# An FFT convolution beside a gated feed-forward net: new buffer homes, a spectrum copied out before it is multiplied, and an order planned with a price on TensorE tile-mode changes

## The chip, the cores and the metric

The kernel runs on one core of a Trainium2 chip. The metric is device time in microseconds (us), the median of several executions; lower is better. The profile shows one execution, engine by engine: PE is TensorE (matmul; PEld its weight loads), DVE is VectorE, ACT is ScalarE, POOL is GpSimd, and SP only issues DMAs here.

## What is computed

S = 2048 rows, D = 640 channels, F = 1728; inputs and outputs are bf16.

```python
xn = layernorm(A_q)                                   # over D
g  = silu(gelu(xn @ B_w1 + B_b1) @ B_w2 + B_b2)       # feed-forward net
k_shift[s] = sum_t A_k[s + t - 3] * A_shift_k[:, 3 - t]   # 4 taps, zero padded in front
kv = k_shift * A_v
y  = irfft(rfft(kv, 2S) * rfft(A_ssm_k, 2S))[:S]      # long convolution over s, per channel
out = A_q + (xn * (y + kv * A_ssm_D)) * g
```

## The kernel before

**Layout.** Row s = 16p + j lies in partition p. The channels are cut into two halves h of 320. Work on rows goes by four chunks c (4 of the 16 j each); the net runs chunk by chunk, the convolution half by half.

**The convolution** is a Fourier transform in two steps, each a matmul against a table of sines.
- `kt` transposes the filter `A_ssm_k` (in `kf_sb`) into `kT` (L580): 16 transposes for each of 5 blocks of 128 channels.
- `f1_pair` (L622) is the first step: two matmuls of 128x320 for each j, against tables WA and WB. It is done for the filter (kinds f1k0, f1k1, from `kT`) and for the product kv (f1u0, f1u1). Each result is evicted to a staging buffer `io` and stored to DRAM (scrK, scrU), from where it comes back regrouped.
- `kv_unit` (L642, L649, L652) makes the product on DVE: for 4 of the 16 j of one half, four multiplies by a tap, three adds, one multiply by V, each 128x1280 in bf16. Its scratch is the tile `GAB`, where the tables of the last step are put later by a DMA transpose (L732). So the tables come after all eight units.
- `middle` (L773, L803, L816) works on 8 groups for each half. `f2k`: the filter's second step, 4 matmuls on 64x64 quarters of the array, twice a group; the result is evicted to `kk`, and a DMA puts a copy with the partitions exchanged beside it (swap, L790). `f2u`: the same for the product, read from `uin`. `prod` (L803): DVE multiplies this spectrum by both versions in `kk`. `i1` (L816): 8 quarter matmuls turn the product back; its result `cs` is evicted and stored to scrC by POOL (L822).
- `last` (L834, L835, L842) loads `cab` from scrC (it waits for all 8 groups of the half), does 4 matmuls of 128x320 and multiplies by xn. `finish` (L539, L541) adds A_q and stores.

**The net.** `layer_norm` (statistics L483, 1/sqrt on POOL L490, normalizing L493), `x_transpose` (DMA transposes, L510), `ffn1` (L522: 5 matmuls of 128x512, gelu on ACT L527; 14 for each chunk), `ffn2` (L557: 14 matmuls of 128x320, silu on ACT L561, multiply into xn on DVE L565; 8 for each chunk).

**Buffers that matter here.** PSUM has two banks `psf` for the net and three double banks `psa` for all else. `w2_sb` shares its memory with `kf_sb`, so w2 is loaded only when all 5 blocks of the filter are transposed:

```python
w2_sb = kf_sb[:].rearrange("p t s -> p (t s)")[:, 0:FT * D]...      # L289
load(ld, F * D * 2, writes=[w2_b], extra=list(kf_b.users), n=3)     # L606
```

`kT` lies over the memory of rows chunks 2 and 3 (`xreg`, L292), so these chunks are loaded when the last filter pair is done. The K and V rows of both halves have homes of their own (`k_all`, `v_all`), which after use serve as `uin`, `cs` and `cab`. The tables' integer scratch lies in `hx[1]`, later the net's second hidden buffer.

**The order.** Every step is recorded as an `op` with its engine, a cost and a kind. `schedule` is a list planner: of the steps that are ready it takes the one that can start first, ties broken by a number for its kind from the table DUE (two numbers a kind, first and last step of it). An eviction may go to ACT or DVE (`"ACT|DVE"`). The steps are then issued in that order, and each engine runs its own in order: a step that waits holds back all behind it on its engine. DMAs are issued by SP in order, too.

Of the kernel before, what the change touches and what calls it, by code (L numbers as in the profile page):

```python
# [9 lines left out]
F32 = mybir.dt.float32  # L10
# [5 lines left out]
P = 128  # L16
# [50 lines left out]
TABLE_LOAD = 1.28  # L67

class Plan:
# [4 lines left out]
    def op(self, eng, cost, fn, reads=(), writes=(), mods=(), hold=(), kind="", table=None, dma=0, rate=360e3, extra=()):  # L74
# [3 lines left out]
        o.fn, o.kind, o.table, o.dma, o.rate = fn, kind, table, dma, rate  # L78
# [33 lines left out]
    def schedule(self):  # L112
# [21 lines left out]
        dma_free, table = 0.0, None  # L134
# [4 lines left out]
        while ready:  # L139
            best = None  # L140
            for o in ready:
# [19 lines left out]
                for e in o.engs:  # L161
# [23 lines left out]
            if e == "ACT" and o.table is not None:  # L185
                table = o.table
            if o.dma:
# [44 lines left out]
def kernel(  # L232
# [119 lines left out]
    def load(fn, nbytes, reads=(), writes=(), extra=(), n=1):  # L352
        nload[0] += 1
        if len(loads) >= 3:
            extra = list(extra) + [loads[-3]]
# [526 lines left out]
```

## Time and profile before

| | |
|---|---|
| median of 3 executions | 227.08 us (226.32 to 228.15) |
| the profiled execution | 226.49 us, span in its profile 224.3 us |
| busy PE / DVE / ACT / POOL | 194.7 / 173.4 / 147.2 / 25.2 us |
| mean granted PE clock | 0.96 |
| moved by DMA | 58.67 MB, 262 GB/s |

The span goes from the first to the last instruction; 2.2 us of the device time lie around it. The text takes a row apart at its first use.

### The profile page before, as it was taken

Reading aid. Unit: us, or ns where it says so; the run is one execution under the profiler, and the core shown is the slowest. Engines: PE = TensorE matmul, PEld = TensorE weight load, DVE = VectorE, ACT = ScalarE, POOL = GpSimd, SP = SyncE. Lnnn points to the kernel's source line nnn. Section 1 sums busy time; section 2 is a strip of 40 time slices with the busy share of each in tenths; the row PEclk is TensorE's granted clock in tenths of the full one; section 3 lists DMA queues with packets and bytes.
Section 4 is the critical chain, followed back from the end, with each engine's and each line's share of the span. In section 5 each row is a group of like instructions: output and inputs, shape, how many; then the busy total and the mean of one; then the engine's idle time right before and its main releaser. Section 6 shows DMA issues by size and latency. Waiting matters only on the chain.

```text
span 224.3 us, 4150 instructions
## 1 busy us (share of the span) xinstructions
PE 194.7 (87%) x1521; PEld 105.5 (47%) x1521; DVE 173.4 (77%) x297; ACT 147.2 (66%) x225; POOL 25.2 (11%) x36
## 2 busy tenths in 40 slices
PE   4523996992899989999999899999899999999992
PEld 1521253541567633446665443343334555657771
DVE  6999989979999978653989666557387697882594
ACT  6397778687278886887766797777646758742110
POOL 8060000002000000110111301110111100220000
PEclk9985599999699999999999999999999999999999
DMA  6999999999995799999959999897999852535953
GB/s 172 358 304 198 303 353 317 377 346 354 225 329 178 250 288 270 267 337 311 346 171 176 262 256 340 245 314 219 294 382 330 248 164 91 177 91 187 358 163 113
DMA packets 63614, 58.67 MB, mean 262 GB/s; under 512 B 17453, under 2 KB 55145, under 8 KB 63594
## 3 DMA queue, kind: packets, MB, share of 16 engines
q1 hardware_dynamic: 62026, 53.16, 81.1%
q0 software_dynamic: 1536, 5.24, 7.3%
q8 instruction: 12, 0.20, 0.4%
q14 instruction: 8, 0.07, 0.1%
q10 hardware_dynamic: 32, 0.01, 0.0%
HBM read 31.14 MB, written 18.35 MB: 221 GB/s over the span
## 4 chain that ended last, share of the span: by engine, by line
PE 67%; DMA 20%; DVE 6%; SPq 2%; ACT 2%; issue 1%; POOL 1%; DVEq 0%; ACTq 0%; POOLq 0%
PE psf_106 L557 14%; PE psf_105 L557 13%; PE psf_105 L522 11%; PE psf_106 L522 10%; DMA w_sb<-in_B_w_dram 5%; DMA kf_sb<-in_B_w_dram 4%; DMA k_all<-scrC_67 3%; DMA kf_sb<-in_A_ssm_k_dram 3%; PE psa_107 L816 2%; PE psa_107 L622 2%; DMA hx_93<-xreg 2%; PE psa_109 L773 2%; PE psa_108 L622 2%; PE psa_108 L773 2%; DMA xreg<-in_A_q_dram 2%; PE psa_109 L622 2%
## 5 line engine op out<-in xcount | busy, mean ns | idle before, releaser
L522 PEld LDWEIGHTS <-w_sb 128*128 128x128 bf16 x280 | 25.3, 99 | 36.2 <-issue 13.1
L557 PEld LDWEIGHTS <-hx_93 128*128 128x128 bf16 x224 | 21.9, 100 | 15.1 <-issue 6.2
L642 DVE TENSOR_TENSOR GAB<-k_all,w_exp 128x1280 bf16<-128x1280 bf16 x32 | 26.0, 820 | 0.5
L557 PEld LDWEIGHTS <-hx_94 128*128 128x128 bf16 x224 | 21.3, 98 | 9.5 <-issue 1.0
L557 PE MATMUL psf_106<-kf_sb,hx_93 128*128 128x320 bf16 x112 | 17.8, 315 | 4.5 <-DMA kf_sb<-in_B_w_dram 4.5
L522 PE MATMUL psf_105<-hx_93,w_sb 128*128 128x512 bf16 x70 | 18.5, 398 | 1.8 <-DMA w_sb<-in_B_w_dram 1.8
L649 DVE TENSOR_TENSOR GAB<-GAB 128x1280 bf16<-128x1280 bf16 x24 | 19.6, 817 | 0.2
L522 PE MATMUL psf_106<-hx_93,w_sb 128*128 128x512 bf16 x70 | 18.5, 397 | 0.9 <-DMA hx_93<-xreg 0.9
L522 PE MATMUL psf_105<-hx_94,w_sb 128*128 128x512 bf16 x70 | 17.5, 380 | 0.5 <-ACT hx_94 L527 0.5
L522 PE MATMUL psf_106<-hx_94,w_sb 128*128 128x512 bf16 x70 | 17.5, 380 | 0.5 <-ACT hx_94 L527 0.5
L557 PE MATMUL psf_105<-kf_sb,hx_93 128*128 128x320 bf16 x112 | 16.6, 300 | 0.0
L557 PE MATMUL psf_106<-kf_sb,hx_94 128*128 128x320 bf16 x112 | 16.6, 299 | 0.0
L557 PE MATMUL psf_105<-kf_sb,hx_94 128*128 128x320 bf16 x112 | 16.6, 299 | 0.0
L483 DVE BATCH_NORM_STATS2 stats<-xreg 128x6 f32<-128x320 bf16 x32 | 13.7, 471 | 2.0 <-DMA xreg<-in_A_q_dram 2.0
L822 POOL DMA_DIRECT2D scrC_67<-v_all x8 | 6.4, 797 | 76.7 <-ACT v_all L313 73.9
L527 ACT ACTIVATE hx_93<-psf_105,b_f 128x512 bf16<-128x512 f32 (+1 forms) x14 | 9.7, 690 | 7.5 <-PE psf_105 L522 7.5
L527 ACT ACTIVATE hx_94<-psf_105,b_f 128x512 bf16<-128x512 f32 (+1 forms) x14 | 9.6, 686 | 7.4 <-PE psf_105 L522 7.3
L622 PEld LDWEIGHTS <-WA 128*128 128x128 bf16 x64 | 6.4, 100 | 13.0 <-ACT WA L452 7.8
L527 ACT ACTIVATE hx_94<-psf_106,b_f 128x512 bf16<-128x512 f32 (+1 forms) x14 | 9.6, 687 | 4.1 <-PE psf_106 L522 3.8
L773 PEld LDWEIGHTS <-F2m 64*64 64x64 bf16 x256 | 6.0, 104 | 13.4 <-issue 12.6
L561 ACT ACTIVATE sl_102<-psf_106 128x320 bf16<-128x320 f32 x6 | 2.6, 437 | 13.7 <-PE psf_106 L557 13.7
L490 POOL TENSOR_TENSOR rstd<-veps,mhalf 128x4 f32<-128x4 f32 x4 | 5.5, 1366 | 51.0 <-DVE veps L487 51.0
(188 smaller groups left out, 405.7 us busy)
## 6 DMA issues: line engine op xcount, KB each, us to landing
kf_sb<-in_A_ssm_k_dram SPq DMA_DIRECT2D x5, 512.0 KB, 6.3
k_all<-in_A_k_dram SPq DMA_DIRECT2D x4, 640.0 KB, 7.9
v_all<-in_A_v_dram SPq DMA_DIRECT2D x4, 640.0 KB, 8.6
kk_95<-kk_95 SPq DMA_DIRECT2D x16, 160.0 KB, 4.4
kk_96<-kk_96 SPq DMA_DIRECT2D x16, 160.0 KB, 3.8
k_all<-scrU_65 SPq DMA_DIRECT2D x8, 320.0 KB, 4.1
scrC_67<-v_all POOLq DMA_DIRECT2D x8, 320.0 KB, 4.6
k_all<-scrU_66 SPq DMA_DIRECT2D x8, 320.0 KB, 5.4
```

Of the source, the lines that this page charges most:

```text
L483: nc.vector.bn_stats(out=stats[:, c, j, h, :], in_=x_b[c].v[:, j, h * H:(h + 1) * H])
L490: op("POOL", 0.96, lambda e: nc.gpsimd.tensor_tensor(out=rstd[:, c, :], in0=veps[:, c, :], in1=mhalf[:], op=ALU.pow), reads=[ve_b[c], mh_b ...
L522: nc.tensor.matmul(out=o, lhsT=w1_sb[:, t, ft * P:(ft + 1) * P], rhs=xnT_b[c].v[:, :, t, :], start=(t == 0), stop=(t == DT - 1))
L527: op("ACT", 0.575, lambda e: nc.scalar.activation(out=hT_b[c].v[0:M, ft, :], in_=ps.v[0:M, :], func=ACT.Gelu_apprx_tanh, bias=b1_f[0:M, ft ...
L557: nc.tensor.matmul(out=ps.v[:, 0:H], lhsT=hT_b[c].v[0:M, ft, q * P:(q + 1) * P], rhs=w2_sb[0:M, ft, hs], start=(ft == 0), stop=(ft == FT - 1))
L561: op("ACT", 0.32, lambda e: nc.scalar.activation(out=sl.v[:], in_=ps.v[:, 0:H], func=ACT.Silu), reads=[ps], writes=[sl], kind="f2_%d" % c, ...
L622: nc.tensor.matmul(out=ps.v[:, c, 0:H], lhsT=W[:, 2 * i + j, :], rhs=src(2 * i + j), start=True, stop=True)
L642: nc.vector.tensor_tensor(out=out_, in0=k_all[:, h, r + 3 - j:r + 3 - j + KR, :], in1=w_exp[:, j, None, hs].to_broadcast([P, KR, H]), op=A ...
L649: op("DVE", 0.735, lambda e, t=t: nc.vector.tensor_tensor(out=a.v, in0=a.v, in1=t.v, op=ALU.add), reads=[t], writes=[a], kind="kv%d" % h)
L773: nc.tensor.matmul(out=ps.v[t * Q:t * Q + Q, u, 0:H], lhsT=W[u * Q:u * Q + Q, :], rhs=src[u * Q:u * Q + Q, 2 * i + t, :], start=True, stop ...
L816: nc.tensor.matmul(out=psc.v[u * Q:u * Q + Q, t, 0:H], lhsT=W[t * Q:t * Q + Q, :], rhs=p12.v[t * Q:t * Q + Q, 2 * a + u, :], start=(a == 0 ...
L822: op("POOL", 1.04, lambda e: nc.gpsimd.dma_start(out=by_group(scrC[h], g), in_=cs.v), reads=[cs], writes=[scrC_b[h][g]], kind="cst%d" % h, ...
```

## The change

1. **Homes.** w2 gets its own memory; the filter `kf_sb` now lies in `hx[1]`, and the tables' integer scratch in w2's. w2's load waits for the tables only. `kT` moves from the rows chunks 2 and 3 to the memory of the second half's K and V (`kv_t[1]`): chunks 2 and 3 may load at any time, and K and V of the second half load only after the last filter pair.
2. **The product's spectrum.** `f2u`'s result is evicted in place into `uin` (ACT or DVE), and `prod` reads it from there in bf16. Before, `prod` read PSUM in f32. `f2u` no longer waits for the swapped filter spectrum, nor for a free staging buffer.
3. **Staging** buffers `io`: 4 for 3.
4. **Normalizing** is x * rstd + (-mean * rstd), with one small DVE step more for each chunk, so that ACT can do it as well as DVE.
5. **The planner** knows PE's tile mode: a change between full-array steps and quarter steps (f2k, f2u, i1) costs 0.095 us and a number of its own in DUE. The costs of some steps, DMA issues above all, are set anew, loads hold one of 3 tokens where they followed the load three before, and all of DUE is new. So the order is new everywhere.

```diff
+MODE_SWITCH = 0.095
...
+                    if e == "PE" and o.mode != mode:
+                        c += MODE_SWITCH
+                        p -= self.due["mode"][0]
...
-    kf_sb = sb.tile([P, DT, S], BF16, name="kf_sb")
-    w2_sb = kf_sb[:].rearrange("p t s -> p (t s)")[:, 0:FT * D].rearrange("p (t d) -> p t d", t=FT)
+    nmr = sb.tile([P, NCH, CH], F32, name="nmr")
+    w2_sb = sb.tile([P, FT, D], BF16, name="w2_sb")
...
-    kT = xreg[:, NCH:].rearrange("p a b d -> p (a b) d")
-    k_all = sb.tile([P, 2, NJ + 3, H], BF16, name="k_all")
-    v_all = sb.tile([P, 2, NJ, H], BF16, name="v_all")
+    kv_t = [sb.tile([P, NK + NJ * H], BF16, name="kv%d" % h) for h in range(2)]
+    kT = kv_t[1][:, 0:NJ * D].rearrange("p (n d) -> p n d", d=D)
...
+    kf_sb = hx[1][:].rearrange("p (t s) -> p t s", t=DT)
...
-    io_t = [sb.tile([P, 4, H], BF16, name="io%d" % i) for i in range(3)]
+    io_t = [sb.tile([P, 4, H], BF16, name="io%d" % i) for i in range(4)]
...
-             writes=[x_b[c]], extra=list(kT_b.users) if c >= 2 else [])
+             writes=[x_b[c]])
...
-             writes=v_b[h].parts[8 * i:8 * i + 8])
+             writes=v_b[h].parts[8 * i:8 * i + 8], extra=list(kT_b.users) if h else [])
...
-        load(ld, F * D * 2, writes=[w2_b], extra=list(kf_b.users), n=3)
+        load(ld, F * D * 2, writes=[w2_b], extra=tab_users, n=3)
...
-            def prod(e, i=i, ps=ps, p12=p12):
-                nc.vector.tensor_tensor(out=p12.v[:].rearrange("p (a u) c -> p a u c", a=2),
-                                        in0=ps.v[:, None, :, 0:H].to_broadcast([P, 2, 2, H]),
-                                        in1=kk.v[:, i], op=ALU.mult)
-
-            op("PE", T2, lambda e, i=i, ps=ps: quads(ps, F2m, uin.v, i), reads=[uin, F2_b, kk], writes=[ps],
-               hold=[p12], kind="f2u%d" % h)
-            op("DVE", 1.4, prod, reads=[ps, kk], writes=[p12], kind="prod%d" % h)
+            op("PE", T2, lambda e, i=i, ps=ps: quads(ps, F2m, uin.v, i), reads=[uin[2], F2_b], writes=[ps],
+               kind="f2u%d" % h, mode=1)
+            op("ACT|DVE", EV, lambda e, i=i, ps=ps: evict(e, uin.v[:, 2 * i:2 * i + 2, :], ps.v[:, :, 0:H]), reads=[ps], writes=[uin[i]],
+               kind="f2u%d" % h)
+
+            def prod(e, i=i, p12=p12):
+                us = uin.v[:, 2 * i:2 * i + 2, :]
+                nc.vector.tensor_tensor(out=p12.v[:].rearrange("p (a u) c -> p a (u c)", a=2),
+                                        in0=us.rearrange("p u c -> p (u c)")[:, None, :].to_broadcast([P, 2, 2 * H]),
+                                        in1=kk.v[:, i].rearrange("p a u c -> p a (u c)"), op=ALU.mult)
+
+            op("DVE", 0.735, prod, reads=[uin[i], kk], writes=[p12], hold=[cs], kind="prod%d" % h)
```

**What moves on the engines.** PE's 274 steps (a step is one recorded group of matmuls) are the same ones. Along its order the tile mode changes 112 times before and 76 times now: quarter steps stand in longer runs between the net's. DVE has 53 casts for 19 (the 34 more are evictions), ACT 111 for 113, and ACT loads its function table 10 times for 12. Three places follow.

SP, the DMA queue, near the start, before: the rows from the last filter block (L372) to the load of the second half's last V piece. `k_all` rows L392 to L394 and `v_all` rows L400 here are the second half's K and V; L384 loads rows chunk 1, L627 stores filter pairs.

```order
17 L372 DMA kf_sb<-in_A_ssm_k_dram 128x2048
18 L392 DMA k_all<-in_A_k_dram 112x3x320
19 L393 DMA k_all<-in_A_k_dram 15x3x320
20 L394 DMA k_all<-in_A_k_dram 128x8x320
21 L380 DMA w_sb<-in_B_w_dram 128x5x576
22 L400 DMA v_all<-in_A_v_dram 128x8x320
23 L627 DMA scrK_63<-io_99 128x1280
24 L627 DMA scrK_63<-io_101 128x1280
25 L394 DMA k_all<-in_A_k_dram 128x8x320
26 L384 DMA xreg<-in_A_q_dram 128x2560
27 L400 DMA v_all<-in_A_v_dram 128x8x320
```

SP in the change: first the same stretch, from the first transposes of xn (L528) to w2 (L623; `kv_91` is the first half's K and V, L394 loads rows chunks 2 and 3).

```order
13 L528 DMA_TRANSPOSE hx_94<-xreg 128x10x128 x2
14 L382 DMA hx_95<-in_A_ssm_k_dram 128x2048
15 L410 DMA kv_91<-in_A_v_dram 128x8x320
16 L394 DMA xreg<-in_A_q_dram 128x2560
...
20 L394 DMA xreg<-in_A_q_dram 128x2560
21 L404 DMA kv_91<-in_A_k_dram 128x8x320
22 L382 DMA hx_95<-in_A_ssm_k_dram 128x2048
23 L646 DMA scrK_63<-io_100 128x1280
24 L646 DMA scrK_63<-io_102 128x1280
25 L623 DMA w_sb<-in_B_w_dram 128x13x640
```

All three pieces of w1 (L390) now stand ahead of this, and w2 stands behind two filter stores whose data are evicted by DVE and ACT. Farther on in SP's order of the change stand the second half's K and V (`kv_92`), around the last store of a filter pair (L646, `scrK_64`):

```order
58 L410 DMA kv_92<-in_A_v_dram 128x8x320
59 L646 DMA scrK_64<-io_101 128x1280
60 L402 DMA kv_92<-in_A_k_dram 112x3x320
61 L403 DMA kv_92<-in_A_k_dram 15x3x320
62 L404 DMA kv_92<-in_A_k_dram 128x8x320
63 L410 DMA kv_92<-in_A_v_dram 128x8x320
```

They have moved from the first fifth of the queue to its middle. On DVE, before, the same multiplies and adds of the second half's first unit stood right behind the first half's, with no work of `middle` between. In the change they stand among products (L830) and evictions (L324) of the first half's `middle`:

```order
157 L324 CAST kv_91<-psa_110 128x640 x2
158 L661 TENSOR_TENSOR GAB<-kv_92,w_exp 128x1280 x3
159 L668 TENSOR_TENSOR GAB<-GAB 128x1280
...
162 L830 TENSOR_TENSOR io_100<-kv_91,kk_96 128x1280
163 L830 TENSOR_TENSOR io_101<-kv_91,kk_96 128x1280
164 L661 TENSOR_TENSOR GAB<-kv_92,w_exp 128x1280
165 L324 CAST kk_96<-psa_108 128x640
...
168 L671 TENSOR_TENSOR kv_92<-GAB,kv_92 128x1280
169 L324 CAST kv_91<-psa_110 128x640
```

From row 158 to the last such multiply, row 211, DVE has 32 instructions of the second half's units, 10 products, 9 evictions and 5 short multiplies of the net (L583).

DVE near the start, in the change: rows chunk 1 is normalized (L508, its statistics some rows ahead) before the second unit of the first half (`kv_91`) begins, and behind it stand the two evictions for the filter stores that w2 follows.

```order
62 L661 TENSOR_TENSOR GAB<-kv_91,w_exp 128x1280
63 L501 SCALAR_TENSOR_TENSOR nmr<-mv,rstd 128x4
64 L671 TENSOR_TENSOR kv_91<-GAB,kv_91 128x1280
65 L508 TENSOR_SCALAR xreg<-xreg,rstd,nmr 128x640 x4
66 L661 TENSOR_TENSOR GAB<-kv_91,w_exp 128x1280
67 L324 CAST io_100<-psa_108 128x640
68 L668 TENSOR_TENSOR GAB<-GAB 128x1280
69 L324 CAST io_102<-psa_110 128x640
```

Before, neither chunk 1's statistics nor an eviction of a pair stood among the first two units:

```order
62 L642 TENSOR_TENSOR GAB<-k_all,w_exp 128x1280
63 L652 TENSOR_TENSOR v_all<-GAB,v_all 128x1280
64 L642 TENSOR_TENSOR GAB<-k_all,w_exp 128x1280
65 L649 TENSOR_TENSOR GAB<-GAB 128x1280
66 L313 COPY xreg<-psa_108 128x8x128
67 L642 TENSOR_TENSOR GAB<-k_all,w_exp 128x1280
68 L649 TENSOR_TENSOR GAB<-GAB 128x1280
```

More of the change, by code (lines that the diff above doesn't have):

```diff
@@ L72, in __init__, with op @@
         self.due = due
-    def op(self, eng, cost, fn, reads=(), writes=(), mods=(), hold=(), kind="", table=None, dma=0, rate=360e3, extra=()):
+    def op(self, eng, cost, fn, reads=(), writes=(), mods=(), hold=(), kind="", table=None, dma=0, rate=360e3, mode=0, extra=()):
         o = Op()
@@ L133, in schedule @@
         free = {"PE": 1.0, "ACT": 1.0, "DVE": 1.0, "POOL": 1.0, "SP": 1.0}
-        dma_free, table = 0.0, None
+        dma_free, table, mode = 0.0, None, 0
         for p in {b.pool for o in ops for b in o.allocs}:
@@ L186, in schedule @@
                 table = o.table
+            if e == "PE":
+                mode = o.mode
             if o.dma:
@@ L594 @@
                reads=[dD_b], writes=[kT_b[2 * u] for u in range(d0 // P, d1 // P)], kind="kt")
-    load_k(1, 0)
-    load_v(1, 0)
+    op("POOL", 0.5, lambda e: nc.gpsimd.memset(hT_t[1][FLAST:FLAST + 1, FT - 1, :], 1.0), writes=[], kind="ones1",
+       extra=list(kf_b.users))
     load_x(1)
+    load_x(2)
+    load_x(3)
     def load_w2():
@@ L666 @@
             f1_pair(i, h, k_src(h), k_dep(h), scrK, scrK_b, "f1k%d" % h)
-    load_x(2)
-    load_x(3)
+    op("POOL", 1.0, lambda e: nc.gpsimd.memset(k_all[1][0:1, 0:3, :], 0.0), writes=[halo_b[1]], kind="halo1",
+       extra=list(kT_b.users))
+    for i in range(2):
+        load_k(1, i)
+        load_v(1, i)
     for h in range(2):
```

96 lines of the change are left out of this document (51 added, 45 removed), and 42 rows, old and new, of the table DUE.

## The prediction

> **What bounds the kernel now.** I read the page first (span, busy times, granted clock), then a table of stages, then PE's waits, then the chain.
>
> ```profile
> span 224.3 us, 4150 instructions
> PE 194.7 (87%) x1521; PEld 105.5 (47%) x1521; DVE 173.4 (77%) x297; ACT 147.2 (66%) x225; POOL 25.2 (11%) x36
> PEclk9985599999699999999999999999999999999999
> ```
>
> ```profile
> 0.00:57.00 57.00, 35.22 (x200) 19.29 (x201) 51.95 (x120) 40.97 (x54) 10.74 (x18) 0.87 1.05 310
> 57.00:224.30 167.30, 159.44 (x1322) 86.25 (x1320) 121.46 (x178) 106.24 (x171) 14.45 (x18) 0.99 0.83 245
> 80.00:140.00 60.00, 58.20 (x480) 28.90 (x479) 42.79 (x69) 45.43 (x74) 6.93 (x8) 1.00 1.00 275
> 57.00:80.00 23.00, 23.00 (x164) 15.05 (x163) 22.24 (x35) 16.29 (x28) 0.00 (x0) 0.95 0.88 240
> 200.00:220.00 20.00, 19.81 (x148) 13.99 (x144) 12.30 (x26) 3.90 (x9) 0.75 (x1) 1.00 0.65 216
> ```
>
> The columns are the stretch, its length, busy PE, PEld, DVE, ACT and POOL with counts, PE clock, DMA share, GB/s. The kernel has two parts. Up to 57 us PE is busy 35 of 57 while DVE (52) and the DMA (share 1.05) are full. After 57 us PE has 159.4 of the 163 us to its last matmul (219.85, below), so it lacks 3.4 us there: what counts is its work and when it starts. PE's waits (who waited <- for whom: us in all, times, longest) and the chain that ended last (start, us, what):
>
> ```profile
> PE psa_108 L622 <- ACT WA L452: 7.7, 1, 7.7
> PE psf_106 L557 <- DMA kf_sb<-in_B_w_dram: 4.5, 1, 4.5
> PE psf_105 L522 <- DMA w_sb<-in_B_w_dram: 1.8, 1, 1.8
> PE psa_108 L834 <- DMA k_all<-scrC_67: 1.6, 2, 1.1
> ```
>
> ```profile
> 46.76 10.05 DMA kf_sb<-in_B_w_dram
> 56.86 3.35 PE psf_106 L557 x14
> 61.03 1.90 PE psf_105 L557 x14
> 66.05 0.14 PE psa_107 L773 x4
> 66.18 2.01 PE psf_105 L557 x14
> 68.19 0.27 PE psa_109 L622 x2
> 87.15 1.19 PE psf_105 L522 x5
> 98.52 1.08 PE psf_105 L522 x5
> 219.85 0.45 ACT sl_103 L561
> 220.68 0.49 DVE xreg L539
> ```
>
> The first ffn2 waits for w2 until 56.86 and runs at a low clock (3.35 us for 1.90; the clock row shows a 6 there). The same step costs 0.11 us more behind quarter steps (1.19 for 1.08, 2.01 for 1.90): the mode change. As a test, all of PE's work behind 56.86 by such rows: 32 ffn2 x 1.90, 42 ffn1 x 1.08, 44 pairs x 0.27, 64 second steps x 0.14, 32 `i1` x 0.27 (twice the matmuls of a second step), 16 `last` x 0.54 (two pairs' worth) make 144.3; 112 changes x 0.11 make 12.3; the low clock 1.45, the idle 3.4. Sum 161.5 against 163.0 in the trace. So PE's side can be priced this way to 1%.
>
> **Part 1, the start.** In both orders 14 ffn1, 5 transposed blocks and 20 pairs stand ahead of the first ffn2. The question is when that is reached.
>
> ```profile
> 13.21 2.87 DVE L493 TENSOR_SCALAR xreg<-xreg,mv,rstd 128x640 bf16<-128x640 bf16 x4 [0.34 <-POOL rstd L490]
> 16.11 4.94 SPq L510 DMA_TRANSPOSE hx_93<-xreg  x2
> 23.61 2.29 PE L522 MATMUL psf_106<-hx_93,w_sb 128*128 128x512 bf16 x5 [0.49 <-DMA hx_93<-xreg]
> 70.10 0.82 DVE L642 TENSOR_TENSOR GAB<-k_all,w_exp 128x1280 bf16<-128x1280 bf16 x1
> 70.95 0.83 DVE L649 TENSOR_TENSOR GAB<-GAB 128x1280 bf16<-128x1280 bf16 x1
> 71.70 0.32 DVE L565 TENSOR_TENSOR xreg<-xreg,sl_103 128x320 bf16<-128x320 bf16 x1
> 8.68 0.83 DVE L483 BATCH_NORM_STATS2 stats<-xreg 128x6 f32<-128x320 bf16 x2
> 9.67 0.20 DVE L708 TENSOR_SCALAR kk_96<-kk_96 128x64 f32<-128x64 f32 x1
> ```
>
> The table's integer steps and small steps stand ahead of the first normalizing in the change; I put it 4 us later (17.3 for 13.2, an estimate from these small rows), so xn's transposes land at about 27.6 for 23.6 and ffn1 starts there. PE's way from there to the first ffn2, by the rows above: 14 ffn1 15.1, 14 pairs 3.8, 2 blocks about 2.4, and 2.3 for a first stretch at the low clock (2.29 for one of the first ffn1): 51.2. DVE's way: normalized at 20.1; then until the evictions ahead of w2 11 multiplies or adds of 0.78 (start to start 0.74 to 0.85 above), four statistics of 1.0 (8.68 to 9.67), a second normalizing (1.5 to 2.9) and 2.4 of small steps: 37 to 38. Second eviction and w2's issue at 39.5; by the 10.05 us above w2 lands at 49.5. The DMA agrees: five pieces of K and V of 640 KB that stood ahead of w2 now stand behind it, and two rows chunks of 640 KB ahead (sizes below), 1.97 MB less, which at the first row's 310 GB/s is 6.3 us. All three pieces of w1 are ahead of xn's transposes in the queue, so the 1.8 us wait for w1 goes; the 7.7 us on table WA stay, the table being made at about the same time. PE is the later of the two; with 0.8 for waits on evictions I take 52.0, **-4.9**. Ends: 49.5 (w2 alone) and 56.9 (nothing won). PE comes to it from continuous work, so the low clock there goes, too: **-1.45**.
>
> **Part 2, mode changes.** 112 to 76, 36 x 0.11 = **-4.0**, all on PE and all behind the first ffn2, where PE has no slack. Ends: nothing, if PE only waits longer elsewhere, and these 4.0.
>
> **Part 3, the product.**
>
> ```profile
> L803 DVE TENSOR_TENSOR io_99<-psa_109,kk_96 128x1280 bf16<-128x1280 f32 x4 | 6.0, 1488 | 1.6 <-PE psa_109 L773 1.6
> L642 DVE TENSOR_TENSOR GAB<-k_all,w_exp 128x1280 bf16<-128x1280 bf16 x32 | 26.0, 820 | 0.5
> L313 DVE CAST v_all<-psa_107 128x640 bf16<-128x640 f32 x3 | 2.5, 824 | 2.7 <-PE psa_107 L816 2.7
> ```
>
> 32 products at 1.49 become 32 at 0.82 (the bf16 row of that size): -21.4 on DVE. The 34 more casts cost 34 x 0.82 = +27.9; two filter evictions less, -1.4; four small steps, +0.8. DVE goes from 173.4 to 179.3 busy us, ACT loses two table loads and little else. PE sees nothing of it as long as DVE keeps up; the PSUM bank comes free after 0.82 for 1.49, the result stays 0.2 later. I cost it at nothing by itself, and take its load into part 4. The fourth staging buffer and the new form of normalizing cost nothing either: all 16 normalizings stay on DVE, under PE's work as before. The Trainium skill, page VectorE: DVE Perf Modes, section Rules for kernel authors, speaks against it: on a matmul's output either accept the slow read from PSUM, or copy first if many operations follow. Here one follows; the rows agree that copy and product, 1.64, cost DVE more than 1.49, and by the rule the sum below would stand higher (the second rival).
>
> **Part 4, the second half's K and V.** They load only behind the last filter pair. Work on PE from the first ffn2 to there: 8 ffn2, 7 ffn1, 28 pairs, 5 quarter steps, 6 changes, 31.7 us: 83.7. Then V and K.
>
> ```profile
> k_all<-in_A_k_dram SPq DMA_DIRECT2D x4, 640.0 KB, 7.9
> v_all<-in_A_v_dram SPq DMA_DIRECT2D x4, 640.0 KB, 8.6
> k_all<-scrU_66 SPq DMA_DIRECT2D x8, 320.0 KB, 5.4
> 82.31 3.99 SPq L732 DMA_TRANSPOSE GAB<-WB  x1
> 86.97 3.17 SPq L732 DMA_TRANSPOSE GAB<-WA  x1
> 81.97 0.83 DVE L652 TENSOR_TENSOR v_all<-GAB,v_all 128x1280 bf16<-128x1280 bf16 x1
> ```
>
> Five issues of about 0.5 (an estimate) and a landing of 7.9 give 94.1. Before, DVE was through with all eight units at 82.8 (last row); now four start at 94.1. With what stands between them (51 instructions x 0.78, 5 x 0.24) they take 41 us if DVE never waits: 135.1. PE reaches the last unit's pairs at 83.7 + 50.3 (27 quarter second steps, 21 ffn1, 14 `i1`, 12 pairs, 7 ffn2, 32 changes) = 134.0: a wait of 1.1. Then SP has two table transposes (7.2) and two stores (1.0) before the last product pair goes out, at 143.3. Store and reload, 5.4 each by the reload's median, end at 154.1; that median holds time in the queue, and I take 153. PE wants the reload after 16.1 us more work, at 134.0 + 1.1 + 16.1 = 151.2: another 1.8. Together **+2.9**, between 0 and, if DVE waits as it did from 80 to 140, far more (below). The 3.4 us of idle that PE had before I leave in.
>
> **Part 5, the tail.**
>
> ```profile
> L842 DVE TENSOR_TENSOR xreg<-psa_108,xreg 128x640 bf16<-128x640 f32 x6 | 4.9, 816 | 0.9 <-PE psa_108 L835 0.9
> ```
>
> PE's order now has 15 `last` steps in the final 19 us, for 8 of them before: at 0.82 each, 14 finishes of 0.49 (chain, last row) and 8 short multiplies of 0.32 that is 21.7 busy us of DVE for 12.3 before, and such instructions overlap by a tenth (0.74 start to start for 0.82). So DVE is just full, and I let it end 0.4 us later behind PE: **+0.4**; ends 0 and 2.7, all that is over 19.
>
> **Sum.** -4.9 - 1.45 - 4.0 + 2.9 + 0.4 = -7.05; 226.49 - 7.05 = **219.4 us** (of the span 217.25 and the 2.2 around it), the profiled execution's 226.49 standing 0.6 under the median of 227.08.
>
> **Rivals.**
> - *DVE sets the pace in the second half (slower).* Place: the four units between 94 and 135. From 80 to 140 DVE was busy 42.8 of 60 us, 71%, since each product waited for PE. At 71% the 41 us become 58, PE waits 17 more and the time is 236. It is slower than before by over 1% when the units take 10 us longer, that is from 80% downward. Against it: in the row 57 to 80 DVE ran at 97% on this mix of units and evictions, with PE never idle.
> - *The copy loses.* A product and the copy of its spectrum take DVE 0.82 + 0.82 for 1.49. If DVE is the bound wherever `middle` runs, 32 x 0.15 = 4.8 comes out of the gain: 224.2. For it: all 34 more evictions stand on DVE. Against it: the 71% above. (By the rule of the Trainium skill's page VectorE: DVE Perf Modes, named in part 3, this is how it goes.)
> - *The start does not move (the change doesn't do what it says).* If the evictions ahead of w2 come as late as DVE's long list allows, or the transposes later than I count, ffn2 starts at 56.9 as before, and waits longer for it, at the low clock. Then only parts 2, 4 and 5 are left: 226.49 - 4.0 + 2.9 + 0.4 = 225.8.
> - *All of it works (faster still).* ffn2 from 50, part 4 at nothing, the 1.6 us that PE waited for the first reloads of `last` gone, since they now stand far ahead of their use: 226.49 - 6.9 - 1.45 - 4.0 - 1.6 + 0.4 = 212.9.
>
> **How the numbers follow.** Forecast 0.50, all works 0.13, copy loses 0.10, start does not move 0.14, DVE sets the pace 0.13. A measurement of this kernel (226.32 to 228.15) tells 1% from no change. Under 224.8 lie the forecast, the fast case and six tenths of the copy's: 0.69. Within 1%: 0.18. Slower: 0.13. The range goes from the fast case to a little over the case in which the start does not move, 212 to 227, and leaves out the slow one and the rims.
>
> **What would show it.** The first ffn2 near 52 us in place of 56.86, at 1.9 us, with its wait on w2 small. ffn2 at 2.01 and ffn1 at 1.19 rarer. Products at about 0.82, DVE's busy time near 179. No hole in PE over 2 us between 100 and 155. I am wrong if PE waits for DVE in the pairs of the second half, or for the product's reload behind the table transposes, or if ffn2 still starts at 57.

## The result, and the profile after

The kernel before took 227.62 us (median of 4; 226.32 to 230.94), the changed one **216.47 us** (median of 4; 215.08 to 218.16). The ratio is 0.9532, 95% interval 0.9435 to 0.9629: 4.7% faster. Medians are taken over all runs of a kernel, ratios over its faster runs alone, those within 1.5% of its fastest. The profiled executions, which all that follows compares, took 226.49 and 215.08 us, 11.4 us apart; 219.4 was forecast.

The page of the changed kernel, its first lines and the row of granted clocks:

```profile
span 212.9 us, 4197 instructions
PE 187.3 (88%) x1521; PEld 106.4 (50%) x1521; DVE 172.8 (81%) x333; ACT 144.8 (68%) x223; POOL 22.1 (10%) x37
PEclk9999799999999999999999999999999999999998
```

PE does the same 1521 matmuls in 7.4 busy us less. The clock row has no low digit from the sixth slice to the tail, where before a 6 stood at the first ffn2. The table of stages of the changed kernel (stretch, length, busy PE, PEld, DVE, ACT, POOL, clock, DMA share, GB/s):

```profile
0.00:48.00 48.00, 32.26 (x200) 18.55 (x200) 42.79 (x112) 37.98 (x49) 6.95 (x18) 0.96 1.06 319
48.00:208.53 160.53, 155.09 (x1324) 87.82 (x1321) 128.88 (x220) 106.43 (x175) 15.15 (x19) 1.00 0.86 267
90.00:100.00 10.00, 7.54 (x46) 3.09 (x46) 6.06 (x9) 6.15 (x10) 1.70 (x2) 1.00 1.10 361
100.00:110.00 10.00, 9.16 (x82) 4.21 (x83) 9.93 (x15) 8.33 (x14) 0.75 (x1) 1.00 1.11 273
110.00:120.00 10.00, 10.00 (x94) 4.58 (x93) 9.98 (x14) 9.86 (x17) 1.51 (x2) 1.00 0.98 336
```

and of the kernel before, from its first ffn2 to its last matmul:

```profile
56.86:219.85 162.99, 159.58 (x1322) 86.35 (x1321) 120.40 (x176) 105.81 (x171) 14.45 (x18) 0.99 0.85 249
```

So the 11.4 us lie in two places. The first ffn2 starts at 48.00 for 56.86: **-8.9**. From there to the last matmul it is 160.5 for 163.0: **-2.5**, made of 4.5 less PE work and 2.0 more waiting (5.4 for 3.4). What follows the last matmul is as before, 4.4 for 4.45 us. PE's waits behind 48 us:

```profile
PE psa_110 L841 <- DVE io_101 L830: 2.0, 1, 2.0
PE psa_109 L794 <- DMA kv_91<-scrU_65: 1.3, 1, 1.3
PE psa_108 L794 <- DMA kv_91<-scrU_66: 0.7, 1, 0.7
PE psa_110 L794 <- DMA kv_91<-scrU_66: 0.4, 1, 0.4
```

The wait on w2 is gone; the new ones are for U's reload and, once, for the product. (Three smaller waits, 0.4 us and less, are left out.) The timeline of the start, by engine (start, us, what, idle before it):

```profile
13.76 1.04 POOL L499 TENSOR_TENSOR rstd<-veps,mhalf 128x4 f32<-128x4 f32 x1 [10.09 <-DVE veps L496]
16.43 1.51 DVE L508 TENSOR_SCALAR xreg<-xreg,rstd,nmr 128x640 bf16<-128x640 bf16 x4
24.77 1.24 PE L540 MATMUL psf_107<-hx_94,w_sb 128*128 128x512 bf16 x5 [0.89 <-DMA hx_94<-xreg]
34.46 0.30 PE L641 MATMUL psa_108<-kv_92,WA 128*128 128x320 bf16 x1 [1.59 <-DVE io_100 L324]
36.32 0.46 SPq L623 DMA_DIRECT2D w_sb<-in_B_w_dram  x1
48.00 0.30 PE L575 MATMUL psf_107<-w_sb,hx_94 128*128 128x320 bf16 x1
```

Rows normalized at 16.4 to 17.9, ffn1 from 24.8, w2 issued at 36.3 for 46.8. And DVE's groups of the second half's units and of the product:

```profile
L661 DVE TENSOR_TENSOR GAB<-kv_92,w_exp 128x1280 bf16<-128x1280 bf16 x16 | 12.9, 818 | 2.8 <-DMA kv_92<-in_A_k_dram 2.7
L830 DVE TENSOR_TENSOR io_103<-kv_91,kk_96 128x1280 bf16<-128x1280 bf16 x7 | 5.7, 819 | 0.3 <-DMA kk_96<-kk_96 0.3
```

The product takes 0.82 us for 1.49, and DVE waits 2.7 us for the late K.

### The profile page after: what moved, and what is told of

It reads as the page before. It is cut to its first block, busy times and chain, and to the rows that moved or that the text cites. A ratio compares the mean times of both kernels' runs of the same rounds, so it can differ in the third digit from the quotient of the medians.

```text
span 212.9 us, 4197 instructions
## 1 busy us (share of the span) xinstructions
PE 187.3 (88%) x1521; PEld 106.4 (50%) x1521; DVE 172.8 (81%) x333; ACT 144.8 (68%) x223; POOL 22.1 (10%) x37
## 4 chain that ended last, share of the span: by engine, by line
PE 55%; DVE 19%; DMA 17%; SPq 3%; issue 2%; ACT 1%; DVEq 0%; ACTq 0%
PE psf_107 L575 10%; PE psf_107 L540 9%; PE psf_106 L575 9%; PE psf_106 L540 9%; DMA kv_91<-scrU_66 8%; DVE GAB L661 5%; DMA hx_95<-in_A_ssm_k_dram 4%; DMA kv_91<-scrU_65 3%; DVE stats L492 3%; DVE GAB L668 3%; DMA kin_98<-scrK_63 2%; DVE xreg L508 2%; PE psa_108 L641 2%; PE psa_110 L794 2%; PE psa_109 L794 1%
## 5 line engine op out<-in xcount | busy, mean ns | idle before, releaser
L540 PE MATMUL psf_107<-hx_94,w_sb 128*128 128x512 bf16 x110 | 27.5, 380 | 0.9 <-DMA hx_94<-xreg 0.9
L575 PEld LDWEIGHTS <-hx_94 128*128 128x128 bf16 x224 | 21.4, 98 | 9.8 <-issue 1.0
L575 PEld LDWEIGHTS <-hx_95 128*128 128x128 bf16 x224 | 21.7, 98 | 9.1 <-issue 0.8
L540 PE MATMUL psf_106<-hx_94,w_sb 128*128 128x512 bf16 x100 | 24.9, 380 | 0.0
L575 PE MATMUL psf_107<-w_sb,hx_94 128*128 128x320 bf16 x112 | 16.7, 300 | 0.2 <-ACT hx_94 L545 0.2
L575 PE MATMUL psf_107<-w_sb,hx_95 128*128 128x320 bf16 x112 | 16.6, 299 | 0.0
L575 PE MATMUL psf_106<-w_sb,hx_94 128*128 128x320 bf16 x112 | 16.6, 299 | 0.0
L575 PE MATMUL psf_106<-w_sb,hx_95 128*128 128x320 bf16 x112 | 16.5, 299 | 0.0
L661 DVE TENSOR_TENSOR GAB<-kv_92,w_exp 128x1280 bf16<-128x1280 bf16 x16 | 12.9, 818 | 2.8 <-DMA kv_92<-in_A_k_dram 2.7
L847 POOL DMA_DIRECT2D scrC_67<-kv_91 x8 | 6.2, 777 | 72.9 <-ACT kv_91 L324 47.1
L794 PEld LDWEIGHTS <-F2m 64*64 64x64 bf16 x256 | 6.1, 105 | 13.5 <-issue 10.1
L661 DVE TENSOR_TENSOR GAB<-kv_91,w_exp 128x1280 bf16<-128x1280 bf16 x16 | 12.6, 799 | 0.0
L545 ACT ACTIVATE hx_94<-psf_107,b_f 128x512 bf16<-128x512 f32 (+1 forms) x15 | 10.4, 692 | 1.8 <-PE psf_107 L540 1.6
L324 ACT CAST kv_91<-psa_109 128x640 bf16<-128x640 f32 x15 | 10.5, 701 | 1.3 <-PE psa_109 L794 1.0
L545 ACT ACTIVATE hx_95<-psf_106,b_f 128x512 bf16<-128x512 f32 (+1 forms) x15 | 10.4, 693 | 1.3 <-PE psf_106 L540 1.0
L598 PEld LDWEIGHTS <-hx_95 128*128 128x128 bf16 x80 | 6.8, 154 | 8.5 <-DMA hx_95<-in_A_ssm_k_dram 8.2
L324 ACT CAST kv_91<-psa_108 128x640 bf16<-128x640 f32 x15 | 10.5, 700 | 0.7 <-PE psa_108 L794 0.7
L545 ACT ACTIVATE hx_95<-psf_107,b_f 128x512 bf16<-128x512 f32 x13 | 9.1, 702 | 2.5 <-PE psf_107 L540 2.5
L545 ACT ACTIVATE hx_94<-psf_106,b_f 128x512 bf16<-128x512 f32 (+1 forms) x13 | 9.1, 697 | 2.5 <-PE psf_106 L540 2.5
```

What stands on the lines that cost most here:

```text
L324: (nc.scalar.copy if e == "ACT" else nc.vector.tensor_copy)(out=out_, in_=in_)
L540: nc.tensor.matmul(out=o, lhsT=w1_sb[:, t, ft * P:(ft + 1) * P], rhs=xnT_b[c].v[:, :, t, :], start=(t == 0), stop=(t == DT - 1))
L545: op("ACT", 0.575, lambda e: nc.scalar.activation(out=hT_b[c].v[0:M, ft, :], in_=ps.v[0:M, :], func=ACT.Gelu_apprx_tanh, bias=b1_f[0:M, ft ...
L575: nc.tensor.matmul(out=ps.v[:, 0:H], lhsT=hT_b[c].v[0:M, ft, q * P:(q + 1) * P], rhs=w2_sb[0:M, ft, hs], start=(ft == 0), stop=(ft == FT - 1))
L598: nc.tensor.transpose(out=o[:, q, :], in_=kf_v[:, t, q, :], identity=ident[:])
L661: nc.vector.tensor_tensor(out=out_, in0=k_all[h][:, r + 3 - j:r + 3 - j + KR, :], in1=w_exp[:, j, None, hs].to_broadcast([P, KR, H]), op=A ...
```

## The experiments

Theory A is the prediction's: PE's work and the moment it can start its unbroken stretch set the time; the homes of w2 and K^T move that moment, fewer mode changes shorten the stretch, the new form of the product costs PE nothing. Its rivals are named in each expectation. Times are medians, each with its ratio to the kernel before. Medians less than 2 us apart are not told from each other here. The kernel before ran again beside each group of runs, with medians of 226.44 to 227.83, so that a difference of medians from two groups can be off by 1.4 us; each ratio is taken within its group. Where an expectation says "fitted anew", the planner's table of numbers was searched again for that structure (small random changes, kept where the planner's own end came earlier).

**Mode changes, their price.** Ahead of each of the 56 ffn1 and 32 ffn2, in the order as it is:

```diff
+            nc.tensor.matmul(out=ps.v[0:n, 0:8], lhsT=hT_b[c].v[0:n, 0, q * P:q * P + n],   # n = 128, then 64
+                             rhs=w2_sb[0:n, 0, 0:8], start=True, stop=True)
             for ft in range(FT):
```

> The changed kernel, its order kept, with one more matmul of 8 columns on the full array (128x128 weights) ahead of each of the 56 ffn1 and 32 ffn2; its result is overwritten by the group that follows. It is the control for the next run and changes no mode. Theory A (PE's own work and its start set the time): 88 times what such a matmul costs PE, 0.02 to 0.06 us, so 2 to 5 us over the changed kernel. Rival B (DVE sets the pace behind 48 us and PE has room): under 1 us.

> The same 88 extra matmuls of 8 columns, but on a quarter of the array (64x64 weights). Where the step ahead is a full one, each adds two mode changes; the emitted order has 182 changes for 76. Theory A with 0.11 us a change: 106 x 0.11 = 11.7 us over the run with the full-array matmuls, and the ffn steps behind a tick at 0.11 more than without. Rival B: PE's extra time goes into its waits, under 4 us over the other run. Rival D (a change costs nothing on PE, and the 0.11 in the rows is how ends are modelled): no difference.

Measured: 218.27 us (ratio 0.9625, 0.9526 to 0.9724) and 221.14 (0.9798, 0.9675 to 0.9922), 2.9 apart; the intervals overlap. The full ticks themselves cost 1.8 over the changed kernel, just under the 2 of theory A and not told from nothing. The same place in both timelines, first with full ticks, then with quarter ticks:

```profile
60.19 0.30 PE L645 MATMUL psa<-kv,WB 128*128 128x320 bf16 x1
60.33 0.17 PE L539 MATMUL psf<-hx,w_sb 128*128 128x8 bf16 x1
60.35 1.24 PE L542 MATMUL psf<-hx,w_sb 128*128 128x512 bf16 x5
```

```profile
60.21 0.30 PE L645 MATMUL psa<-kv,WB 128*128 128x320 bf16 x1
60.44 0.19 PE L539 MATMUL psf<-hx,w_sb 64*64 64x8 bf16 x1
60.56 1.25 PE L542 MATMUL psf<-hx,w_sb 128*128 128x512 bf16 x5
```

From start to start the full tick costs 0.16 us from the pair to ffn1, the quarter tick 0.35: 0.19 more for two changes, **0.095 each**. So it is at all 53 ticks that stand behind a full-array step: by kind of that step the medians are 0.18 to 0.19 apart. The changed kernel's own rows agree: from the start of a 320-column matmul to that of the next step it is 0.229 with a change and 0.136 without. Rival D is out: a change is real time on PE. But 106 x 0.095 = 10.1 us of it made the kernel only 2.9 longer. The stretches from the first ffn2 to the last matmul, full ticks, then quarter ticks:

```profile
47.87:211.74 163.87, 158.33 (x1398) 89.68 (x1395) 128.78 (x219) 106.50 (x175) 15.12 (x19) 0.99 0.84 262
```

```profile
48.94:214.60 165.66, 162.97 (x1397) 91.84 (x1396) 127.58 (x216) 105.78 (x175) 14.90 (x19) 1.00 0.81 256
```

Busy time rises by 4.6 and PE's idle time falls from 5.5 to 2.7. (78 of the changes lie in the stretch, 7.4 us. Two things bring that near the 4.6: behind a quarter step the quarter tick is 0.04 quicker than the full one, 0.229 for 0.267 us from start to start, 1.3 over 35 such ticks; and the clock, 0.99 for 1.00, may be some 1.6.) That the waits for DVE and for reloads end at moments which PE's extra work does not move, so that it fills them, fits these rows; it was not tested by itself. Theory A's 11.7 is wrong as a price on the time, though right to 15% as a price on PE.

**w2 issued late.** The order as it is, but w2 ahead of the second chunk's transposes and behind a small transfer that waits for a filter block:

```diff
+            nc.sync.dma_start(out=scrC[1][0:1, 0:8], in_=kT[1:2, 7, D - 8:D])   # w2_late2: kT[1:2, 15, 384:392]
             nc.sync.dma_start(out=w2_sb[:, 0:FT - 1, :], ...)
```

> The changed kernel, its order kept, but w2's load is put behind the first eviction of the last transposed filter block, which is where its old home among the filters would have had it: one 16-byte transfer out of that block makes SP wait, and w2 stands just behind it, ahead of the second chunk's transposes. Issue at about 41.4 for 36.3. Theory A (the gain of the start is when w2 is there, and each microsecond of it comes out at the end): the first ffn2 at 51 to 53 for 48.0, PE waiting on w2 for 3 to 4.5 us, the whole 3 to 6 us longer. Rival C (the start is not what counts, since the second half's K and V, DVE or the stores set the end): first ffn2 later, the whole within 1 us.

> As w2_late, but the 16 bytes that SP waits for now come out of the block that is transposed last (39.3 us in the changed kernel); in w2_late they came out of one that was evicted by 29 us, so that w2's issue moved by only about 1 us. Issue at about 42 for 36.3, landing 10.4 to 11 us later, at 52 to 53. Theory A: first ffn2 at 52 to 53, PE waiting 4 to 5 us for w2, partly at a low clock behind it; the whole 4 to 6.5 us over the changed kernel, 220 to 223. Rival C (something behind the start sets the end): within 1 us of the changed kernel.

Measured: 217.32 us (212.95 to 219.27, too wide for a ratio) and 218.61 (ratio 0.9567, 0.947 to 0.9664). The first of the two moved w2's issue by only 1.5 us, to 37.9, so it doesn't do what was expected of it; its first ffn2 starts at 48.86, behind a wait of 1.5 for w2. Timeline of the second:

```profile
41.69 0.39 SPq L629 DMA_DIRECT2D w_sb<-in_B_w_dram  x1
50.18 3.97 PE L580 MATMUL psf<-w_sb,hx 128*128 128x320 bf16 x28 [2.18 <-DMA w_sb<-in_B_w_dram]
```

w2 goes out 5.4 us later, lands in 8.4 for 10.4, and the first ffn2 comes 2.2 later, by a wait of 2.2. So in the changed kernel w2 landed (36.3 + 10.4) some 1.3 us ahead of its use, and when it comes later it is what the first ffn2 waits for: theory A's mechanism, at half the size for the start. What it does to the whole is not shown: the median is 2.1 higher, but the two ratios, 0.9567 and the changed kernel's 0.9532, are not told apart.

**The first normalizing late.** Four multiplies of DVE inside it:

```diff
             def norm(e, j=j):
+                if c == 0 and j == 0:
+                    for _ in range(4):
+                        nc.vector.tensor_tensor(out=<1280 columns of GAB>, in0=..., in1=..., op=ALU.mult)
```

> The changed kernel, its order kept, with four multiplies of 0.82 us (into a region that is overwritten later) ahead of the first normalizing on DVE, which moves it from 16.4 to 19.7 us: that is where the prediction had put it too late by 2.8 us. Theory A (ffn1 follows the first normalizing, and PE's way from there to the first ffn2 is full): first ffn2 at 50.5 to 51.5 for 48.0, the whole 2 to 3.5 us longer, 218.5 to 220. Rival J (w2's landing, at 47.2, sets it, and PE's way has room): first ffn2 by 49, the whole within 1 us.

Three of the four normalizings still ran at 16.4; the multiplies stand ahead of the fourth, which xn's transposes wait for. Measured: 221.88 us (ratio 0.9835, 0.9655 to 1.0015), 5.4 over the changed kernel. The timeline and the stages of it:

```profile
17.47 3.39 DVE L509 TENSOR_TENSOR GAB<-xreg 128x1280 bf16<-128x1280 bf16 x4
37.74 0.30 PE L646 MATMUL psa<-kv,WA 128*128 128x320 bf16 x1 [2.11 <-DVE io L324]
52.96 0.30 PE L580 MATMUL psf<-w_sb,hx 128*128 128x320 bf16 x1
```

```profile
36.00:38.00 2.00, 0.26 (x2) 0.19 (x2) 2.00 (x4) 0.39 (x1) 0.00 (x0) 1.00 1.13 385
38.00:40.00 2.00, 2.00 (x10) 0.98 (x8) 2.00 (x4) 1.11 (x2) 0.00 (x0) 0.71 0.84 335
40.00:42.00 2.00, 2.00 (x6) 0.63 (x5) 1.97 (x5) 0.86 (x2) 0.00 (x0) 0.50 0.94 261
```

3.3 us more on DVE move the eviction that PE waits for by 3.3 (34.46 to 37.74) and w2's issue, behind the stores, by 3.3 (to 39.6); the first ffn2 comes 5.0 later, the last 1.7 by a clock of 0.71 and 0.50 behind the wait, which theory A's 50.5 to 51.5 and its 3.5 at most did not have. It reaches the end: the profiled execution's span is 7.4 longer, 5.0 in the start and 2.4 behind it. Rival J is out, as the first ffn2 comes late without a wait for w2. So it is DVE's list that sets the start, through the transposes and the evictions that PE waits for.

**The second half's units lighter.**

```diff
-            op("DVE", 0.735, lambda e, j=j, t=t: mul(t.v, j), ...)
+            op("DVE", 0.735, lambda e, j=j, t=t: None if h and j == 3 else mul(t.v, j), ...)   # and its addition
```

> The changed kernel, its order kept, without one tap (a multiply and an addition) in the four second-half units; that part of the computation is left out. DVE has 8 instructions of 0.82 us less, 6.6 us, in the stretch from about 95 to 138 us. Theory A: PE lacks about 5 us behind 48 us, of which 2 to 3 wait on DVE's results there; the whole gets 0 to 2.5 us shorter. Rival B (DVE sets the pace there): 5 to 6.6 us shorter.

Measured: 215.85 us (ratio 0.953, 0.9452 to 0.9609): no difference from 216.47, with 5.7 us less on DVE (167.1 for 172.8). PE's waits moved to other causes. Rival B's 5 to 6.6 us did not come: DVE does not set the pace there.

**The parts alone.** Three kernels take one thing back or do one thing alone, a fourth gives only the planner; all are fitted anew.

```diff
kT_home       -    kT = kv_t[1][:, 0:NJ * D]...                 +    kT = xreg[:, NCH:]...
three_buffers -    ... for i in range(4)]                       +    ... for i in range(3)]
w2_home       -    w2_sb = sb.tile([P, FT, D], ...)             +    w2_sb = <the filters' tile>, filters apart from hx[1], 3 buffers
```

> The changed kernel with K^T back in its old home, the region of the rows' chunks 2 and 3: these chunks load behind the last filter pair, the second half's K and V are free from the start. The planner's table is fitted anew to this structure. 86 mode changes for 76. Theory A with part 4 of the prediction as it came out (the new home costs 1.8 us of waits): 1 to 3 us faster by that, 1.0 slower by the changes, so 213.5 to 217.5. Rival E (the new home is what lets w2 come early, since otherwise five pieces of K and V want to be ahead of it): first ffn2 2 us later or more, the whole 2 to 5 us slower, 218 to 222.

Measured: 217.77 us (ratio 0.9632, 0.9568 to 0.9696). The first ffn2 stands at 51.42, 3.4 later, as rival E says, but the stretch is shorter than in the changed kernel:

```profile
51.42:211.07 159.65, 156.00 (x1322) 86.93 (x1322) 129.65 (x221) 106.11 (x175) 14.36 (x18) 1.00 0.85 262
```

PE lacks 3.7 us in it, for 5.4. K^T's home buys a start and pays for part of it with late K and V: +1.3 us in all, between the ranges of theory A and rival E and not told from nothing.

> The changed kernel with 3 staging buffers for 4, the table fitted anew. 82 mode changes for 76, 0.6 us. The prediction put the fourth buffer at nothing: 215.5 to 218. Rival F (stages wait for a buffer, so the fourth is what hides the copy of U): PE's waits on the product and on staging 3 us more, 219 to 222.

Measured: 218.32 us (ratio 0.9647, 0.9573 to 0.972), 1.9 over the changed kernel. Start at 47.04, stretch 164.95, of which 6.1 idle, 4.4 on U's reload. The prediction's 218 at most is passed by 0.3, rival F's 219 is not reached: not resolved.

> The changed kernel with w2 back in the filters' region (issued only behind the last transposed filter block) and the sine tables' scratch back in the second ffn buffer; for room it has 3 staging buffers, so three_buffers (218.3) is what it is held against. 90 mode changes for 82, 0.8 us. Theory A: first ffn2 at 51 to 54, the whole 2.5 to 6 us over three_buffers, 221 to 224. Rival I (K and V of the second half being out of the queue is what brings w2 early, not its home): first ffn2 by 50, within 1.5 us of three_buffers.

Measured: 220.0 us (ratio 0.9711, 0.9482 to 0.9941), 1.7 over three_buffers. First ffn2 at 49.89, behind a wait of 2.4 for w2, for 47.04. Between theory A and rival I, and too near for either; by the profile the home is worth some 2.9 us of start.

> The kernel before (old homes, product from PSUM, 3 buffers) with the changed kernel's planner: it knows the mode change and the newer durations, and its table is fitted anew to this structure. 100 mode changes for 112. Theory A (the homes carry the start, and the start carries most): first ffn2 at 53 to 57, 1.2 us from the changes, so 223 to 226. Rival C (the newly fitted order alone brings it, the homes little): 216 to 219.

Measured: 226.9 us (ratio 1.0015, 0.9959 to 1.0072): as the kernel before. The first ffn2 of it waits as before:

```profile
57.72 3.91 PE L565 MATMUL psf<-kf_sb,hx 128*128 128x320 bf16 x14 [4.44 <-DMA kf_sb<-in_B_w_dram]
```

Rival C, the order alone, is out. Theory A's 1.2 us from 12 fewer changes did not show either.

**The form of the product.** In the changed kernel back to the old form, and in the kernel before the new form alone:

```diff
-            op("ACT|DVE", EV, lambda e, ...: evict(e, uin.v[:, 2 * i:2 * i + 2, :], ps.v[:, :, 0:H]), ...)
-            op("DVE", 0.735, prod, reads=[uin[i], kk], ...)      # in0 from uin
+            op("DVE", 1.4, prod, reads=[ps, kk], ...)            # in0 from ps
```

> The changed kernel with the old form of the product: U's spectrum is not evicted, the product reads it out of PSUM. All new homes and 4 buffers stay; the table is fitted anew. 102 mode changes for 76, at the 0.095 us that the ticks showed 2.5 us. Theory A with part 3 of the prediction (the form of the product is worth nothing to PE): 216.5 to 220. Rival H (the copy costs DVE more than the old form): 212 to 216. Rival G (the short product out of SBUF carries the stretch behind 48 us, since PSUM banks come free earlier and DVE's chain per group is shorter): 220.5 to 226.

> The kernel before with its old homes and 3 buffers, but U's spectrum evicted in place and multiplied from SBUF; the planner knows the mode change, the table is fitted anew. 80 mode changes for 112, 3.0 us. order_alone (226.9, 100 changes) is the same without the product's new form. Theory A: the start stays at 56 to 58, 1.9 us come from the changes: 223 to 226. Rival G: 216 to 221.

Measured: 224.25 us (ratio 0.996, 0.9892 to 1.0028) and 221.06 us (ratio 0.9807, 0.9688 to 0.9926). With order_alone and the changed kernel they make a square (median us; first ffn2; from it to the last matmul; of that idle; mode changes in the emitted order):

| | old homes, 3 buffers | new homes, 4 buffers |
|---|---|---|
| product from PSUM | order_alone 226.9; 57.72; 162.0; 2.4; 100 | prod_psum 224.25; 48.43; 167.9; 9.3; 102 |
| U evicted, product from SBUF | product_alone 221.06; 55.06; 160.8; 4.7; 80 | changed kernel 216.47; 48.00; 160.5; 5.4; 76 |

The new form is worth 5.8 us with the old homes and 7.8 with the new ones; in each column the two intervals of the ratio lie apart (0.9959 to 1.0072 against 0.9688 to 0.9926; 0.9892 to 1.0028 against 0.9435 to 0.9629). By the ratios the two are 4.7 and 9.7 us: the gain is shown in both columns, its size is known to some 3 us, and that it is larger with the new homes is not shown. The homes and the fourth buffer are worth 2.7 with the old form (1.2 by the ratios), not told from nothing, and 4.6 with the new one (6.2). With them go the new form of normalizing and the loads' tokens, which no run takes apart. By its times rival G holds, product_alone 0.06 above its range; theory A's part 3 and rival H fall. What the old form does to the new homes, in prod_psum: the stretch, PE's waits behind 48 us, and the product's group on DVE:

```profile
48.43:216.35 167.92, 158.62 (x1320) 85.81 (x1317) 129.42 (x174) 100.64 (x165) 14.00 (x18) 1.00 0.83 254
```

```profile
PE psa L856 <- DMA kv<-scrC: 4.9, 5, 1.4
PE psa L838 <- DVE io L827: 2.0, 3, 0.8
PE psa L795 <- DVE io L827: 0.9, 2, 0.7
```

```profile
L827 DVE TENSOR_TENSOR io<-psa,kk 128x1280 bf16<-128x1280 f32 x32 | 46.8, 1485 | 11.4 <-DMA kk<-kk 5.2 <-PE psa L795 4.7 <-issue 1.5
```

The start is won here too (48.43) and lost again: 7.4 us more in the stretch. 3.5 of them are busy time (26 more changes are 2.5 of that), 3.9 are idle: PE waits for the product, and five times for the reloads of `last`, as if the chain of groups ran late. With the old homes it goes another way. The same group in order_alone, and the group with one of the copies in product_alone:

```profile
L811 DVE TENSOR_TENSOR io<-psa,kk 128x1280 bf16<-128x1280 f32 x32 | 47.2, 1488 | 17.5 <-PE psa L781 15.6 <-ACT sl L569 1.7
```

```profile
L818 DVE TENSOR_TENSOR io<-k_all,kk 128x1280 bf16<-128x1280 bf16 x32 | 25.4, 821 | 11.0 <-DMA kk<-kk 7.3 <-PE psa L829 3.1 <-ACT k_all L322 0.3
L322 DVE CAST k_all<-psa 128x640 bf16<-128x640 f32 x9 | 7.4, 823 | 6.9 <-PE psa L782 4.3 <-ACT hx L536 2.6
```

DVE stood idle for 17.5 us ahead of the products, 15.6 of them for PE; now it is 11.0, 7.3 of them for the swapped filter spectrum and 3.1 for PE. 23 of the 32 copies went to ACT, so that DVE's busy time falls from 172.1 to 166.1. The freed order then gives a first ffn2 at 55.06 for 57.72, without a wait for w2, and a stretch 1.2 shorter. That room on DVE is what the order turns into time, in one column as start, in the other as fewer waits, fits these rows; it was not tested by itself. One caution: each order is the end of a search, and no run shows how near it is to the best for its structure. A better order for prod_psum would take something off the 7.8. In the old column the old form has two orders of different tables, the kernel before and order_alone, and both came out alike (ratio 1.0015), which speaks against one bad search there.

No version that does the whole work came out faster than the changed kernel.

## Why the prediction was right, and where not

The time was forecast 2.9 us too high (219.4 for 216.47); sign and place were right. By its own steps:

- **The start** was right in its mechanism and too small: -8.9 for -4.9, outside its ends (49.5 to 56.9). The term that was mis-sized is the first normalizing: I put it at 17.3 to 20.1, it ran at 16.4 to 17.9, four of them in 1.51 us for the 2.87 that I took over from before, where one of them ran beside a POOL step (last section). ffn1 started at 24.77 for my 27.6; PE's way from there was 23.2, waits and all, for my 23.6 and 0.8. w2 went out at 36.3 for my 39.5, the evictions ahead of it having come earlier by as much. norm_late shows that this chain is the one: 3.3 us on DVE there moved the first ffn2 by 5.0. The PE wait that I kept (7.7 on table WA) became 5.8 on a filter; the pairs started at 20.48 for 20.40.
- **The low clock** at the first ffn2 went, as forecast. That it can come back behind a wait is shown by order_alone (3.91 us for that step, behind 4.4) and norm_late.
- **Mode changes**: 0.095 us each for my 0.11, so 3.4 for 4.0 of PE's work; the stretch lost 4.5 of busy time with the clock's 1.45. But the step from PE's work to the time failed: at the margin 106 changes cost 2.9, some 0.03 each, since PE's waits took in the rest. I had named that as the lower end ("nothing, if PE only waits longer elsewhere") and taken the upper one, with "where PE has no slack"; there were 3 to 5 us of it.
- **The product** is the step that was wrong in kind: "PE sees nothing of it" was costed at nothing, and it is worth 5.8 to 7.8 us. I compared DVE's sums for one product (0.82 + 0.82 for 1.49) as if DVE had to do both; the planner may give the copy to ACT, a copied spectrum (by the code) frees its bank without waiting for K's swap, and 20 to 26 fewer mode changes come with it. The forecast was near all the same, since I had put the gain on the start, where the profile shows it; that what the start wins reaches the end only with the new product is shown by prod_psum, which starts at 48.43 and takes 224.25. So the nearness of the number is in part luck: a step put at nothing was worth more than any term of the sum, and the start came out 4.0 larger than forecast. DVE's busy time came to 172.8 for my 179.3: I had added durations, where busy time counts overlapping instructions once (start to start 0.74 for 0.82): the durations of DVE's instructions in the two traces add up to 188.4 and 192.4, 4.0 more, while busy time fell by 0.7.
- **The late K and V**: PE waits 2.0 us more behind the first ffn2, for my 2.9, but mostly not where I had put it. The first unit began at 93.3, as forecast (94.1). The second half's pairs, which I had waiting 1.1, did not wait. The last product pair's store went out at 139.5 for my 143.3, and its reload was waited for by 0.4 us for my 1.8. The two long waits lie in the first half's `middle`, while K and V of the second half load (DMA share 1.10 from 90 to 100): 1.3 for a reload of U that went out at 88.85, right behind four transfers of K and V (82.8 to 88.7), and 2.0 for a product. That K and V in the queue delay these fits, and kT_home, which has K and V early, waits 0.3 for U's reload; but the order there is another one, and no run changes this alone.

```profile
88.85 2.36 SPq L816 DMA_DIRECT2D kv_91<-scrU_65  x1
95.75 0.33 PE L794 MATMUL psa_109<-kv_91,F2m 64*64 64x320 bf16 x4 [1.33 <-DMA kv_91<-scrU_65]
100.84 0.33 PE L841 MATMUL psa_110<-io_101,I1a 64*64 64x320 bf16 x4 [1.97 <-DVE io_101 L830]
139.47 0.53 SPq L646 DMA_DIRECT2D scrU_66<-io_100  x1
146.41 2.28 SPq L816 DMA_DIRECT2D kv_91<-scrU_66  x3
152.56 0.33 PE L794 MATMUL psa_110<-kv_91,F2m 64*64 64x320 bf16 x4 [0.39 <-DMA kv_91<-scrU_66]
```

- **The tail** moved by nothing, for my +0.4.
- **The rivals.** "DVE sets the pace" is out by kv_light; "the start does not move" is out by the first ffn2 at 48.00. "The copy loses" is out by the square. That rival was also the rule of the Trainium skill, VectorE: DVE Perf Modes, section Rules for kernel authors, which advises a copy first only where many operations follow. One follows here, and copying first was the faster form in both columns; the measurement decides.

Summed over the profiled executions: start -8.9, clock -1.45, changes -3.4 to -4.0, waits +2.0, tail -0.1 make -11.9 to -12.5 against -11.4 measured; 0.5 to 1.1 us of PE work is left unexplained.

## What to carry to other kernels

Where a gain shows in the trace is not which edit made it: when an order is planned anew, an edit that costs "nothing" can be the one that lets the rest be kept, and a square of two parts, each with its own fitted order, tells it in four runs. An engine that is 97% busy still has waits, and here work put on it was first paid out of these: price a term on PE's work and on the time apart. Evicting a matmul's result on whichever engine is free and multiplying from SBUF can beat reading it once out of PSUM, as it did here twice; that few banks and a product that is a link of a chain are the reason was not tested.

## What was not expected of the hardware

Behind a wait of 2.1 us on PE the clock fell in norm_late (0.71, then 0.50 for 2 us); behind waits of 2.2 in w2_late2 and 2.4 in w2_home it did not (their first two ffn2 took 3.97 and 3.98 us, full speed). So the length of one wait does not decide it. The Trainium skill, page TensorE: Matmul & The Clock Gate, section What's actually happening, has the clock fall behind an idle window of about 3.4 us whose place is not tied to the kernel; the free place would explain why like waits differ, though none was that long.

The four first normalizings took 1.51 us, and 2.87 before, where a POOL memset ran beside them; a step on the identity took POOL 0.29 us, and 2.39 before, where DVE's 2048-column multiply (2.56 to 4.85) ran beside it. POOL's timeline of the kernel before, then of the changed one:

```profile
2.60 2.39 POOL masks.py:199 TENSOR_SCALAR_AFFINE_SELECT ident<-ident 128x128 bf16<-128x128 bf16 x1
13.15 1.69 POOL L440 MEMSET k_all<- 1x1920 bf16 x1
```

```profile
1.91 0.29 POOL masks.py:199 TENSOR_SCALAR_AFFINE_SELECT ident<-ident 128x128 bf16<-128x128 bf16 x1
```

The normalizings of the kernel before, all 16 (shortest, median and longest in ns):

```profile
L493 DVE TENSOR_SCALAR xreg<-xreg,mv,rstd x16: 428/441/1803, 13.2 to 126.3; 128x640 bf16<-128x640 bf16 x16
```

The long one is the first, which began with the memset. product_alone, with the same instruction, has 1.80 us for the one that began at 17.78, beside a memset from 17.71 to 19.40; in order_alone, again with the same instruction, the memset was over at 19.35, the first normalizing began at 19.55 and took 0.44. The step on the identity took 2.25 to 2.39 us where DVE's multiply ran beside it (in the kernel before, order_alone, product_alone and prod_psum), and 0.29 in the changed kernel and tick_full, where it was over before the multiply began. So each of these two steps takes longer beside the other engine's; which of the two engines waits, and for what, no run here tested.
